# Turning queries and keys in 32x32 blocks on VectorE, with cluster masks placed by small transfers, in a routed-attention and feed-forward kernel

## The chip, the cores and the metric

The kernel runs on one core of a Trainium2 chip. The metric is device time in microseconds (us) of one execution. A profile of one execution shows five engines: PE (TensorE, matmuls; its weight loads are shown apart as PEld), DVE (VectorE), ACT (ScalarE), POOL (GpSimd) and SP (SyncE, which here only issues transfers). Each engine runs its own instructions strictly in the order in which the program lists them, and waits on semaphores for the others.

## The reference

Queries, keys and values have 4 batches, 8 heads, 768 tokens and 64 features. Each head has 16 cluster centroids; a query sees only keys of its own cluster. Behind the attention stands a feed-forward layer over 3072 tokens with a hard-swish gate.

```python
q_assign = np.argmax(np.einsum('bhsd,hcd->bhsc', q_n, c_n), axis=-1)
k_assign = np.argmax(np.einsum('bhsd,hcd->bhsc', k_n, c_n), axis=-1)
mask = q_assign[:, :, :, None] == k_assign[:, :, None, :]
scores = np.where(mask, scale * np.matmul(q, k.transpose(0, 1, 3, 2)), -1e9)
attn = softmax(scores);  x = np.matmul(attn, v)          # heads side by side: (3072, 512)
h = x @ w_in;  y = (h * np.clip(h + 3.0, 0.0, 6.0) / 6.0) @ w_out
```

## The kernel before

**Pairs of heads.** The 32 heads are worked on as 16 pairs `g` = 0 to 15 (two heads of one batch, 128 feature rows). Pairs 0 to 6 are computed as full attention (`FIRST` is 7, the eighth pair; `SECOND` is 8, the ninth). From pair 7 on, tokens are sorted by cluster and only a band of the scores is computed; those pairs are worked in between the feed-forward matmuls, from about 217 us on.

**The first stage** is a loop over `n`, in steps of two, of 12 key blocks for each of the seven pairs (`r = n % 12`). For each `n`, `scores` puts the masked scores of two heads into PSUM, by an f32 matmul on the turned data `xf` and a bf16 matmul on the mask `xm`; the first `n` of a pair starts with `xf`, all others with `xm`. `exponentials` (ACT) makes `ex`, `key_sums` adds these up in `acc` (POOL, in three places DVE), and `attn_v` multiplies with the values. `sum_up` (`pd`, at the third step of the next pair) sums `acc` over partitions.

**Preparing the next pair** is spread over the steps of the present one (`prep_items`). At `r` = 0 and 2, `turn` transposes queries and keys, loaded as tokens by features (`qk`), on PE: twelve 128x128 transposes into PSUM, copied to `xf` by ACT. At `r` = 4, `cluster_scores` (`pcs`) multiplies with the centroids, and ACT copies the result to `cs`. At `r` = 6, `route` turns `cs` on PE (`pr`, three transposes), and DVE takes the maximum (`mx`) and marks where it stands (`one_hot`). At `r` = 8 and 10, `route_turn` turns the marks back on PE (`po`, six bf16 transposes each) and ACT writes the mask `xm`. `count` (ACT) adds up the marks for a check of ties. The pairs 7 and 8 are turned in this stage too (`turn(FIRST, ...)` at `n` = 18 to 22; pair 8 at `n` = 72 and 74), with `own_clusters` and `order` in place of the masks.

**Weights.** The weights come as 64-bit floats, in 32 chunks of 512 KB (`raw`, three buffers). Each takes five DVE steps, one after another (L249, L255, L265, L271, L276), and two on ACT. They fill the rest of DVE: the list `decode` (160 such steps and four `weight_sums`) is worked off in portions that the function `share(n, r)` states for each step of the loop, after that step's preparation. A portion later in the list only starts when what stands ahead of it on DVE is done.

**The end of the stage.** From `n` = 64 on, the first feed-forward block runs too (`ph`, L660; ACT and DVE make the gate `g_sb` from it). At `n` = 84, `order(SECOND)` puts ranks into PSUM (`rk`), DVE multiplies them (L1142), and PE's next `pd` takes the same PSUM buffer.

**Queues.** The order on every engine is the order in which the program states it. SP issues the loads of `qk` (`load`, at `r` = 6), of values (`r` = 8), of weights, and the writes of the attention result (`xd<-num`). `qk` has one buffer. In the late stage, `load_natural` and `turn_blocks` already load and turn in blocks of 32x32: `rearrange` lets a transfer place 32x32 pieces such that DVE's transpose, which works on each block of 32x32 by itself, gives the whole turned matrix.

Of the kernel before, what the change touches and what calls it, by code (L numbers as in the profile page):

```python
# [8 lines left out]
F32 = mybir.dt.float32  # L9
# [8 lines left out]
C = 16  # L18
# [107 lines left out]
def fast_path(ctx, tc, ok, q, k, v, centroids, moe_w_in, moe_w_out, out):  # L126
# [44 lines left out]
    half_c = const.tile([P, 1], F32, name="half_c")  # L171
    cnT = const.tile([P, H * C], F32, name="cnT")
    one_hot = nump.tile([P, NC2, P], BF16, name="one_hot")


    plain = const.tile([P, FIRST * 2 * NCH], F32, name="plain")
# [20 lines left out]

    def load(g, *names):  # L200
        if g > FIRST or (g == FIRST and "v" in names):
            return
        if g == FIRST:
            g = SECOND
        b, h = divmod(2 * g, H)
        for name in names:
            if name == "v":
                dst = st["v", g] = vp.tile([P, 2, NCH, D], F32, name="vt")
            elif name == "q":
                if g == 1:  # L210
                    st["qk", g] = spare_rows(0)
                else:
                    st["qk", g] = qkp.tile([P, 2, NCH, 2, D], F32, name="qk")
            if name != "v":
                dst = st["qk", g][:, "qk".index(name)]
            src = {"q": q, "k": k, "v": v}[name]
            for t in range(2):
                queue = nc.scalar if (g, name, t) == (0, "q", 1) else nc.sync
                queue.dma_start((dst[:, t] if name == "v" else dst[:, :, t]), src[b, h + t].rearrange("(p j) d -> p j d", p=P))
# [103 lines left out]


    def turn(g, part, bank=None, held=None):
        if part == 0 and g == FIRST:
            st["xf", g] = spare[:, 2 * NC2 * P : 3 * NC2 * P].rearrange("p (n c) -> p n c", n=NC2)
        elif part == 0:
            st["xf", g] = xp.tile([P, NC2, P], F32, name="xf")
        qk, xf = st["qk", g], st["xf", g]  # L330
        pt = bank if bank is not None else scratch([P, 4, P], "pqk")
        for i in range(4):
            j = part * 4 + i
            if g == 0 and j == NCH:

                centroid_turn()
            nc.tensor.transpose(out=pt[:, i], in_=qk[:, j // NCH, j % NCH], identity=ident)
        dst = xf[:, part * 4 : part * 4 + 4]

        if g == 0 and part == 2:  # L340
            nc.vector.tensor_copy(out=dst, in_=pt)
        elif held is not None:
            held.append(lambda: nc.scalar.copy(out=dst, in_=pt))
        else:
            nc.scalar.copy(out=dst, in_=pt)
        if part == 2:
            st.pop(("qk", g))
# [4 lines left out]
    def cluster_scores(g):  # L352
        c0, xf = (2 * g) % H * C, st["xf", g]
        ps = scratch([P, 512], "pcs")[:, 0 : NC2 // 4 * P]
        for a in range(4):
            nc.tensor.matmul(  # L356
                ps[a * 2 * C : (a + 1) * 2 * C], lhsT=cnT[:, c0 : c0 + 2 * C], rhs=xf[:, a::4],
                start=True, stop=True,
            )
# [5 lines left out]
        nc.scalar.copy(out=cs, in_=ps)  # L365

    def route(g):
# [25 lines left out]

        later.append(count)

    def route_turn(g, part):
        if part == 0:
            st["xm", g] = xp.tile([P, NC2, P], BF16, name="xm")
        xm = st["xm", g]
        po = scratch([P, NCH, P], "po", BF16)  # L400
        for i in range(NCH):
            nc.tensor.transpose(out=po[:, i], in_=one_hot[:, part * NCH + i], identity=ident_q)
# [601 lines left out]
    Q = 32  # L1004

    def new_blocks(key):
        piece = st[key] = st["piecep"].tile([P, S], F32, name="piece")
        return piece

    def load_natural(g, a):  # L1010
        b, h = divmod(2 * g, H)
        blocks = new_blocks(("nat", g, a))
        for t in range(2):
            rows_ = (q, k)[a][b, h + t].rearrange("(r j c) (x i) -> x j c r i", j=Q, c=NCH, i=Q)
            for x in range(2):
                at = (2 * t + x) * Q
                nc.sync.dma_start(
                    blocks[at : at + Q].rearrange("p (c r i) -> p c r i", c=NCH, i=Q), rows_[x]
                )

    def load_sorted(g, a):
        blocks = new_blocks(("sorted", g, a))
# [414 lines left out]
    def prep_items(g, r):  # L1437

        if g > FIRST:
            return []  # L1440
        if g == FIRST:
            g = SECOND
        turns = [lambda part=part: turn(g, part) for part in range(3)]
        if g == SECOND:
            return {
                0: turns[:2], 2: turns[2:], 4: [lambda: cluster_scores(g)], 6: [lambda: own_clusters(g)],
            }.get(r, [])
        one_hots = [lambda: route_turn(g, 0), lambda: route_turn(g, 1)]
# [33 lines left out]
    def load_first():  # L1482
        b, h = divmod(2 * FIRST, H)
        st["qk", FIRST] = spare_rows(1)
        for a, x in enumerate((q, k)):
            for t in range(2):
                nc.sync.dma_start(st["qk", FIRST][:, a, :, t], x[b, h + t].rearrange("(p j) d -> p j d", p=P))
# [31 lines left out]
    with tc.manual_schedule():  # L1519
# [4 lines left out]
        load(0, "v")  # L1524
        load_weights(0)
        centroid_norm()
        for part in range(3):
            turn(0, part)
        idle(4)
# [14 lines left out]
        for n in range(0, total + lag_d + 2, 2):  # L1544
# [437 lines left out]
```

## Time and profile before

| what | value |
|---|---|
| median of 3 runs | 918.08 us (916.83 to 923.38) |
| the profiled execution | 917.25 us, of which the profile's span is 915.4 us |
| PE, PEld busy | 894.2 us (98%), 700.7 us (77%) |
| DVE, ACT, POOL busy | 581.9 us (64%), 304.2 us (33%), 602.9 us (66%) |
| seven pairs of the first stage | about 14 to 217 us |

A line of the windows view gives, for a stretch of the span, each engine's busy time with its count of instructions, then PE's granted clock (1.00 is full), the mean busy share of the DMA engines, and GB/s. A line of the timeline gives start, duration (of merged instructions, from the first to the last), engine, source line, operation and tiles. A line of the groups gives the busy time of a group, the mean duration of one instruction in ns, and the idle time just ahead of them with what ended it.

### The profile page before, as it was taken

How to read it: one execution, taken by the hardware profiler on the slowest of the kernel's cores; microseconds unless marked ns; L12 is line 12 of the kernel's file. 1: busy time of each engine (PE TensorE's matmuls, PEld its weight loads, DVE VectorE, ACT ScalarE, POOL GpSimd, SP SyncE). 2: the span in 40 equal slices, each digit the busy share in tenths (PEclk: the TensorE clock that was granted, in tenths of full speed). 3: DMA queues.
4: the chain of work that ended last, by engine and by line, in shares of the span. 5: the costliest groups of instructions: out<-in, count | busy, mean ns of one | idle time of the engine just before them, and what ended most of it. 6: DMA issues, size and time to landing. Idle time of an engine off the chain costs nothing.

```text
span 915.4 us, 17376 instructions
## 1 busy us (share of the span) xinstructions
PE 894.2 (98%) x6131; PEld 700.7 (77%) x6131; DVE 581.9 (64%) x1326; ACT 304.2 (33%) x627; POOL 602.9 (66%) x1438
## 2 busy tenths in 40 slices
PE   8999999997999999999999999999999999999997
PEld 5444445555788788797897887978978899999996
DVE  6775899777778378285594674765763645447461
ACT  6888786751221221322222131230321412112120
POOL 3877899995847848878878877788788461202030
PEclk9999999998999999999999999999999999999999
DMA  7756686526578467685785773965726344233210
GB/s 180 185 142 172 176 208 189 158 78 135 156 200 178 130 161 159 150 201 136 175 214 115 180 190 100 216 158 130 189 91 144 93 108 123 77 89 97 68 43 28
DMA packets 248249, 130.92 MB, mean 143 GB/s; under 512 B 206972, under 2 KB 225688, under 8 KB 248152
## 3 DMA queue, kind: packets, MB, share of 16 engines
q1 hardware_dynamic: 224184, 81.22, 37.0%
q10 hardware_dynamic: 13600, 34.31, 13.2%
q0 software_dynamic: 10368, 14.18, 5.0%
q8 instruction: 51, 0.84, 0.4%
q14 instruction: 46, 0.38, 0.1%
HBM read 99.69 MB, written 29.97 MB: 142 GB/s over the span
## 4 chain that ended last, share of the span: by engine, by line
PE 56%; DVE 4%; DMA 1%; issue 1%; another core or an unknown queue 0%; POOL 0%; ACT 0%; ACTq 0%
PE Y L758 15%; PE uY L719 13%; PE X L758 10%; PE uX L719 10%; PE pv L1300 2%; PE ps L1243 2%; PE pv L1243 1%; DVE g_sb L730 1%; DVE g_sb L541 1%; DVE sx L730 1%; PE pd L1324 1%; PE ps L1052 1%; PE pcs L356 1%; PE ps L1341 1%; DMA kvn<-in_k_dram 0%
## 5 line engine op out<-in xcount | busy, mean ns | idle before, releaser
L1213 POOL DMA_INDIRECT xn<-xsd,pos x108 | 109.5, 1014 | 59.1 <-PE uY L719 16.9
L538 ACT ACTIVATE sx<-g_sb,half_c 128x512 f32<-128x512 f32 x88 | 63.7, 724 | 199.6 <-DVE g_sb L730 160.7
L1162 POOL MEMSET unread<- 128x1 f32 x972 | 102.7, 106 | 37.6
L457 POOL TENSOR_TENSOR acc<-acc,ex 128x768 f32<-128x768 f32 x56 | 104.7, 1870 | 16.6 <-ACT ex L446 14.1
L1170 POOL DMA_INDIRECT qd<-qn,pos x96 | 99.2, 1034 | 19.9 <-issue 15.7
L703 POOL TENSOR_TENSOR g_sb<-g_sb 128x256 f32<-128x256 f32 x52 | 38.6, 764 | 111.0 <-DVE g_sb L541 110.0
L1170 POOL DMA_INDIRECT kvd<-kvn,pos x96 | 96.1, 1001 | 21.4 <-issue 21.4
L758 PE MATMUL X<-w_out_sb,g_sb 128*128 128x256 f32 x384 | 93.6, 388 | 1.5 <-issue 0.7
L719 PE MATMUL uX<-xb,w_in_sb 128*128 128x128 f32 x704 | 93.0, 275 | 0.0
L758 PE MATMUL Y<-T,g_sb 128*128 128x256 f32 x384 | 88.5, 381 | 0.0
L758 PE MATMUL Y<-w_out_sb,g_sb 128*128 128x256 f32 x384 | 88.4, 381 | 0.0
L719 PEld LDWEIGHTS uX<-xb,w_in_sb 128*128 128x128 f32 x704 | 85.7, 192 | 0.0
L758 PEld LDWEIGHTS X<-w_out_sb,g_sb 128*128 128x128 f32 x384 | 71.6, 193 | 17.2 <-issue 6.2
L758 PEld LDWEIGHTS Y<-w_out_sb,g_sb 128*128 128x128 f32 x384 | 72.1, 190 | 12.6 <-issue 2.7
L758 PEld LDWEIGHTS Y<-T,g_sb 128*128 128x128 f32 x384 | 71.9, 190 | 12.4 <-issue 2.7
L730 DVE TENSOR_TENSOR sx<-uX,sx 128x128 f32<-128x128 f32 x176 | 50.8, 288 | 42.5 <-ACT sx L737 30.4
L765 DVE TENSOR_TENSOR y<-y,Y 128x256 f32<-128x256 f32 x47 | 19.8, 421 | 86.1 <-PE Y L758 72.0
L423 PE MATMUL ps<-xf 64*128 64x384 f32 x336 | 68.8, 487 | 0.7 <-ACT ex L446 0.7
L730 DVE TENSOR_TENSOR g_sb<-uY,sx 128x128 f32<-128x128 f32 (+1 forms) x176 | 65.6, 414 | 0.0
L541 DVE SCALAR_TENSOR_TENSOR g_sb<-sx,g_sb 128x512 f32<-128x512 f32 x88 | 63.7, 726 | 2.0 <-ACT sx L538 1.0
L446 ACT ACTIVATE ex<-ps 128x768 f32<-128x768 f32 x84 | 63.7, 803 | 3.1 <-PE ps L423 2.6
L467 PE MATMUL pv<-ex,vt 128*64 128x384 f32 x336 | 63.5, 499 | 0.0
(230 smaller groups left out, 1717.8 us busy)
## 6 DMA issues: line engine op xcount, KB each, us to landing
tx<-td ACTq DMA_DIRECT2D x86, 384.0 KB
raw<-in_moe_w_in_dram SPq DMA_DIRECT2D x16, 512.0 KB
raw<-in_moe_w_out_dram SPq DMA_DIRECT2D x16, 512.0 KB
out_dram<-y SPq DMA_DIRECT2D x45, 128.0 KB
xb<-xd SPq DMA_DIRECT2D x11, 512.0 KB
piece<-qd SPq DMA_DIRECT2D x36, 96.0 KB
piece<-kvd SPq DMA_DIRECT2D x36, 96.0 KB
vs<-kvd SPq DMA_DIRECT2D x18, 192.0 KB
```

Source lines behind the costliest of these rows:

```text
L423: nc.tensor.matmul(st["ps", n][:, t, 0:HALF], lhsT=x[r, NCH + j], rhs=x[r, hf * NHC : (hf + 1) * NHC], start=first, stop=last, skip_group_ ...
L446: nc.scalar.activation(out=ex, in_=sc, func=ACT.Exp, scale=SM_SCALE)
L457: nc.gpsimd.tensor_tensor(out=acc, in0=acc, in1=ex, op=ALU.add)
L467: nc.tensor.matmul(pv[t * D : (t + 1) * D], lhsT=vt[:, t, j], rhs=ex[:, t], start=(j == 0), stop=(j == NCH - 1),)
L538: nc.scalar.activation(out=r, in_=h, func=ACT.Relu, bias=half_c, scale=1.0 / 6.0)
L541: nc.vector.scalar_tensor_tensor(out=g, in0=r, scalar=1.0, in1=h, op0=ALU.min, op1=ALU.mult)
L719: nc.tensor.matmul(dst, lhsT=w[:, kt], rhs=x(kt), start=(kt == 0), stop=(kt == HK - 1))
L730: nc.vector.tensor_tensor(out=out_, in0=in0, in1=in1, op=ALU.add)
L758: nc.tensor.matmul(bank[:, half * HC : (half + 1) * HC], lhsT=g_sb[:, kind, i], rhs=w[:, i], start=(first and i == 0), stop=(last and i == ...
L1162: nc.gpsimd.memset(unread, 0.0)
L1170: i = nc.gpsimd.indirect_dma_start(out=rows[name, g, t], in_=src[:, j, t].rearrange("p a d -> p (a d)") if a else src[:, j, t], in_offset= ...
L1213: nc.gpsimd.indirect_dma_start(out=xn[:, j, t], out_offset=None, in_=rows["xsd", g, t], in_offset=bass.IndirectOffsetOnAxis(ap=pos[:, 0, j ...
```

## The change

For pairs 2 to 8, queries and keys are loaded in 32x32 pieces (four transfers each for queries and for keys, of 768 pieces of 128 bytes, in place of two of 768 pieces of 256 bytes) and turned by one DVE instruction each, in place of twelve PE transposes and three ACT copies. For pairs 1 to 6, the cluster scores are turned by DVE (five instructions, with the maximum and the marks between them), and the mask goes from the work buffer `cs` into `xm` by eight small transfers on SP's queue, at `r` = 8. The mask buffers `xm` become two fixed ones, cleared once; queries load at `r` = 6 and keys at `r` = 8. The portions of weight decoding change: one step more in each of the pairs 0, 1 and 2 and two more in pair 3, five fewer in pair 6. Pair 0 is worked as before, and pair 1's queries and keys are still turned by PE.

```diff
+    def in_blocks(piece, g, a):
+        b, h = divmod(2 * g, H)
+        for t in range(2):
+            rows_ = (q, k)[a][b, h + t].rearrange("(r j c) (x i) -> x j c r i", j=Q, c=NCH, i=Q)
+            for x in range(2):
+                at = (2 * t + x) * Q
+                nc.sync.dma_start(
+                    piece[at : at + Q].rearrange("p (c r i) -> p c r i", c=NCH, i=Q), rows_[x]
+                )
+    def turn_early(g, a):
...
+        dst = st["xf", g][:, a * NCH : (a + 1) * NCH]
+        nc.vector.transpose(out=dst.rearrange("p j c -> p (j c)"), in_=st["qk", g][:, a])
...
     def cluster_scores(g):
...
-                ps[a * 2 * C : (a + 1) * 2 * C], lhsT=cnT[:, c0 : c0 + 2 * C], rhs=xf[:, a::4],
+                ps[a * 2 * C : (a + 1) * 2 * C], lhsT=cnT[:, c0 : c0 + 2 * C], rhs=part,
...
+    def mask_constants():
+        nc.gpsimd.memset(xms[1], 0.0)
+        nc.gpsimd.memset(counts[:, 1, 1:FIRST], -NC2 * (C - 1.0))
...
+    def block_route(g):
+        n = NC2 // 4 * P
+        cs = st.pop(("cs", g)).rearrange("p i c -> p (i c)")
+        by_token, oh = (
+            one_hot.rearrange("p j c -> p (j c)").bitcast(F32)[:, i * n : (i + 1) * n]
+            .rearrange("p (i c) -> p i c", c=C) for i in range(2)
+        )
+        nc.vector.transpose(out=by_token.rearrange("p i c -> p (i c)"), in_=cs)
+        mx = rtp.tile([P, n // C], F32, name="mx")
+        nc.vector.reduce_max(out=mx, in_=by_token, axis=AX.X)
+        nc.vector.tensor_tensor(
+            out=oh, in0=by_token, in1=mx.unsqueeze(2).to_broadcast([P, n // C, C]), op=ALU.is_ge
+        )
+        nc.vector.transpose(
+            out=by_token.rearrange("p i c -> p (i c)"), in_=oh.rearrange("p i c -> p (i c)")
+        )
+        ms, seen = (cs.bitcast(BF16)[:, i * n : (i + 1) * n] for i in range(2))
+        st["ms", g] = ms.rearrange("p (i c) -> p i c", c=P)
+        nc.vector.tensor_scalar(
+            out=ms, in0=by_token.rearrange("p i c -> p (i c)"),
+            scalar1=own[:, 0:1], scalar2=own[:, 1:2], op0=ALU.mult, op1=ALU.add,
+        )
...
+    def place_masks(g):
+        ms, xm = st.pop(("ms", g)), xms[g % 2]
+        st["xm", g] = xm
+        for a in range(4):
+            for t in range(2):
+                nc.sync.dma_start(
+                    xm[t * D : t * D + C, a // 2 * NCH : (a // 2 + 1) * NCH][:, a % 2 :: 2],
+                    ms[(2 * a + t) * C : (2 * a + t + 1) * C],
+                )
...
         return {
-            0: turns[:2], 2: turns[2:], 4: [lambda: cluster_scores(g)], 6: [lambda: route(g)],
-            8: one_hots[:1], 10: one_hots[1:],
+            0: turns[:1], 2: turns[1:], 4: [lambda: cluster_scores(g)], 6: [lambda: block_route(g)],
+            8: [lambda: place_masks(g)],
         }.get(r, [])
...
     def share(n, r):
         if n < 36:
-            return {0: 4, 2: 4, 4: 4, 6: 1, 8: 3, 10: 4}[r]
+            return {0: 4, 2: 4, 4: 4, 6: 1, 8: 4, 10: 4}[r]
         if n < 48:
-            return {0: 3, 2: 4, 4: 1, 6: 2, 8: 5, 10: 5}[r]
+            return {0: 4, 2: 4, 4: 2, 6: 2, 8: 5, 10: 5}[r]
...
-        return {0: 6, 2: 6, 4: 5, 6: 2, 8: 5, 10: 5}[r]
+        return {0: 6, 2: 6, 4: 4, 6: 2, 8: 4, 10: 2}[r]
...
     ranking = {
-        8: [load_first], 18: [lambda: turn(FIRST, 0)], 20: [lambda: turn(FIRST, 1)], 22: [lambda: turn(FIRST, 2)],
+        10: [lambda: load_first(0)], 14: [lambda: load_first(1)],
+        20: [lambda: turn_early(FIRST, 0)], 22: [lambda: turn_early(FIRST, 1)],
...
             if r == (4 if g == NKT else 6):
-                load(g + 2, "q", "k")
+                load(g + 2, "q")
             if r == 8:
                 load(g + 1, "v")
+                load(g + 2, "k")
```

More of the change, by code (lines that the diff above doesn't have):

```diff
@@ L173, in fast_path @@
     one_hot = nump.tile([P, NC2, P], BF16, name="one_hot")
+    xms = [nump.tile([P, NC2, P], BF16, name=f"xm{i}") for i in range(2)]
+    own = const.tile([P, 2], F32, name="own")
     plain = const.tile([P, FIRST * 2 * NCH], F32, name="plain")
@@ L325, in turn @@
     def turn(g, part, bank=None, held=None):
-        if part == 0 and g == FIRST:
-            st["xf", g] = spare[:, 2 * NC2 * P : 3 * NC2 * P].rearrange("p (n c) -> p n c", n=NC2)
-        elif part == 0:
+        if part == 0:
             st["xf", g] = xp.tile([P, NC2, P], F32, name="xf")
@@ L394, in route, with count @@
         later.append(count)
+    def mask_constants():
+        nc.gpsimd.memset(xms[1], 0.0)
+        nc.gpsimd.memset(counts[:, 1, 1:FIRST], -NC2 * (C - 1.0))
+        for a, (scale, bias) in enumerate(((1.0, 0.0), (FAR, -FAR))):
+            nc.gpsimd.memset(own[a * D : (a + 1) * D, 0:1], scale)
+            nc.gpsimd.memset(own[a * D : (a + 1) * D, 1:2], bias)
+    def block_route(g):
[20 more added lines that the diff above has]
+        )
+        def count():
+            nc.scalar.activation(
+                out=seen, in_=oh.rearrange("p i c -> p (i c)"), func=ACT.Copy, scale=0.5, accum_out=counts[:, 0, g : g + 1],
+            )
+        later.append(count)
+    def place_masks(g):
[6 more added lines that the diff above has]
+                    ms[(2 * a + t) * C : (2 * a + t + 1) * C],
+                )
     def route_turn(g, part):
         if part == 0:
-            st["xm", g] = xp.tile([P, NC2, P], BF16, name="xm")
+            st["xm", g] = xms[0]
         xm = st["xm", g]
@@ L1010, in load_natural @@
     def load_natural(g, a):
[L1011 to L1019, printed above, removed]
+        in_blocks(new_blocks(("nat", g, a)), g, a)
     def load_sorted(g, a):
@@ L1442, in prep_items @@
             g = SECOND
-        turns = [lambda part=part: turn(g, part) for part in range(3)]
+        turns = [lambda a=a: turn_early(g, a) for a in range(2)]
         if g == SECOND:
             return {
-                0: turns[:2], 2: turns[2:], 4: [lambda: cluster_scores(g)], 6: [lambda: own_clusters(g)],
+                0: turns[:1], 2: turns[1:], 4: [lambda: cluster_scores(g)], 6: [lambda: own_clusters(g)],
             }.get(r, [])
-        one_hots = [lambda: route_turn(g, 0), lambda: route_turn(g, 1)]
         if g == 1:
```

29 lines of the change are left out of this document (21 added, 8 removed).

## The prediction

> **What bounds the kernel now.** First the page's engine lines, then windows cut at the pairs' first masked scores, then who waited for whom.
>
> ```profile
> span 915.4 us, 17376 instructions
> PE 894.2 (98%) x6131; PEld 700.7 (77%) x6131; DVE 581.9 (64%) x1326; ACT 304.2 (33%) x627; POOL 602.9 (66%) x1438
> ...
> 34.10:58.60 24.50, 24.50 (x173) 11.54 (x175) 16.70 (x25) 20.79 (x43) 18.31 (x11) 1.00 0.66 185
> 58.60:83.80 25.20, 25.20 (x180) 11.00 (x178) 13.19 (x20) 21.69 (x45) 20.60 (x17) 1.00 0.51 147
> 83.80:109.10 25.30, 24.52 (x175) 10.86 (x171) 23.71 (x41) 19.55 (x40) 20.93 (x22) 1.00 0.57 158
> 109.10:133.80 24.70, 23.85 (x163) 10.35 (x163) 22.00 (x29) 21.67 (x46) 22.47 (x36) 1.00 0.66 182
> 133.80:169.40 35.60, 34.80 (x211) 19.71 (x211) 31.56 (x44) 24.35 (x53) 33.32 (x44) 1.00 0.71 199
> 211.60:216.20 4.60, 0.00 (x1) 0.03 (x1) 4.57 (x7) 0.11 (x1) 0.44 (x2) 0.94 0.84 210
> 216.20:222.50 6.30, 6.30 (x20) 4.08 (x21) 6.16 (x15) 0.48 (x1) 4.09 (x4) 0.50 0.43 106
> ```
>
> The five long rows are pairs 1 to 5. PE (first number behind the length) fills them to 97% and more, so PE bounds this stage and what it loses moves the end. But DVE (third) is at 22.0 of 24.7 us in pair 4 and 31.6 of 35.6 in pair 5: only pairs 1 and 2 have room. The last two rows are the stage's end: PE stands still for 4.6 us and then runs at half its clock for 6.3 us. DVE's own waits up to 182 us:
>
> ```profile
> DVE mx L374 <- PE pr L371: 15.3, 3, 7.2
> DVE g_sb L541 <- ACT g_sb L538: 5.5, 3, 2.5
> DVE mx L1074 <- PE pr L1072: 4.3, 1, 4.3
> DVE acc L454 <- ACT ex L446: 2.0, 2, 1.2
> DVE wtop L249 <- ACT xf L343: 0.4, 1, 0.4
> DVE acc L454 <- issue: 0.3, 1, 0.3
> ```
>
> Together 27.8 us (total, times, longest). More work than that cannot hide on DVE, as its order is fixed.
>
> **What PE loses.** From start to next start in the timeline of PE:
>
> ```profile
> 86.26 1.09 PE L337 MATMUL pqk<-ident,qk 128*128 128x128 f32 x8
> 87.29 0.34 PE L423 MATMUL ps<-xm 64*128 64x384 bf16 x2
> ...
> 91.23 0.66 PE L337 MATMUL pqk<-ident,qk 128*128 128x128 f32 x4
> 91.82 0.34 PE L423 MATMUL ps<-xm 64*128 64x384 bf16 x2
> ...
> 99.65 0.55 PE L371 MATMUL pr<-ident,cs 128*128 128x128 f32 x3
> 100.14 0.34 PE L423 MATMUL ps<-xm 64*128 64x384 bf16 x2
> ...
> 103.30 0.51 PE L402 MATMUL po<-ident_q,one_hot 128*128 128x128 bf16 x6
> 103.74 0.34 PE L423 MATMUL ps<-xm 64*128 64x384 bf16 x2
> ```
>
> Turning a pair takes 1.03 + 0.59 = 1.62 us, its clusters and masks 0.49 + 2 x 0.44 = 1.37 us. Seven turns and six masks: 11.3 + 8.2 = 19.5 us off PE. Nothing is added there: `cluster_scores` reads other columns, but as many.
>
> **What DVE gains.** Prices from the groups of DVE:
>
> ```profile
> L271 DVE SCALAR_TENSOR_TENSOR wunit<-raw,wunit 128x512 f32<-128x512 uint32 x32 | 35.7, 1117 | 1.0
> L265 DVE TENSOR_SCALAR wunit<-wtop 128x512 uint32<-128x512 uint32 x32 | 22.0, 689 | 0.8
> L380 DVE TENSOR_TENSOR one_hot<-pr,mx 128x192 bf16<-128x192 f32 x12 | 3.7, 353 | 0.4
> L374 DVE TENSOR_REDUCE mx<-pr 128x24 f32<-128x384 f32 x6 | 3.3, 554 | 15.4 <-PE pr L371 15.3
> L1080 DVE TENSOR_TENSOR oh<-pr,mx 128x384 bf16<-128x384 f32 x2 | 1.1, 558 | 0.1
> L1030 DVE STREAM_TRANSPOSE xsort<-piece 128x768 f32<-128x768 f32 x18 | 17.2, 965 | 9.8 <-DMA piece<-qd 5.6 <-DMA piece<-kvd 4.1
> ```
>
> - Turns: two transposes of 128x768 for each of seven pairs, the operation of L1030: 14 x (0.965 + 0.03 between instructions) = 13.9 us.
> - Masks: five instructions on 128x384, each near L1080's and L374's 0.56 us; the last, which the trace lacks, I take as 0.4. That makes 2.6 us, 2.7 with the gaps. L271, the decoding step that reads two SBUF tensors, averages 1.12 us where L265 takes 0.69; it stretches while POOL adds up `acc`. I take two such delays of 0.43 for each mask (the comparison reads two SBUF tensors; the scaling I count too): 3.6 us. Bounds: 2.7 without delay, 2.7 + 5 x 0.43 = 4.9 with one on each instruction. It replaces 0.55 + 2 x 0.35 = 1.3 us. Net 2.3 (1.4 to 3.6) each, six times 13.8 us (8.4 to 21.6).
> - Decoding steps brought ahead of pair 6: three in pairs 0 to 2, two in pair 3. A step averages (4 x 0.69 + 1.12)/5 + 0.03 = 0.81 us (the other three steps stand at 0.68 to 0.70 in the timeline lines below): 4.0 us.
>
> [...]
>
> **The sum.** PE meets DVE in each pair at two places: `pcs` needs the turned data, and the next pair's first scores need the masks. All of DVE's additions stand ahead of the turned keys of the ninth pair (`n` = 74), which PE needs for its last `pcs`:
>
> ```profile
> 181.07 0.69 DVE L249 TENSOR_SCALAR wtop<-raw 128x512 uint32<-128x512 uint32 x1
> ...
> 184.12 0.85 PE L356 MATMUL pcs<-xf,cnT 128*32 128x384 f32 x8
> ...
> 206.06 0.68 DVE L276 TENSOR_TENSOR w_out_sb<-wtop,wunit 128x512 f32<-128x512 f32 x1
> ...
> 207.51 0.70 DVE L255 SCALAR_TENSOR_TENSOR wtop<-raw,wtop 128x512 uint32<-128x512 uint32 x1
> ...
> 215.51 0.55 DVE L1142 TENSOR_TENSOR y<-rk,oh 128x384 f32<-128x384 f32 x1
> 216.20 1.51 PE L493 MATMUL pd<-acc,ones 128*32 128x384 f32 x8 [4.60 <-DVE y L1142]
> ```
>
> DVE ended the step that will stand just ahead of that transpose at 181.8 us. Without its waits that is 154.0; with 13.9 + 13.8 + 4.0 it is 185.7. PE alone would be there at 184.1 - 19.5 = 164.6. So DVE takes PE's place as the bound of the first 185 us, and the ninth pair's `pcs` comes at about 185.8: 1.7 us **later** than before. PE's 19.5 us go into waits at `pcs` and at the masks.
>
> Behind that, DVE has five decoding steps less and waits for PE again, so the last stretch stays with PE. Four of the five stood ahead of L1142, which kept PE waiting until 216.2: 4 x 0.7 = 2.8 us less, so the gap of 4.6 shrinks to about 1.8. The clock fell about 4.0 us after PE had stopped (in the 4.6 us row the mean is 0.94: half rate in its last 0.55 us). A gap of 1.8 ends before that, and the 6.3 us at 0.50 take 3.1 us less. [...]
>
> In all +1.7 - 2.8 - 3.1 = -4.2: 917.25 becomes 913.0 for this profiled execution; it lies 0.8 under the median of the runs, so I say **914 us**.
>
> **What lies beside.** ACT only loses copies, and has room in every row. POOL clears `xm` once at the start, before it has sums to add. The piece loads move the same 0.79 MB per pair in twice the pieces; rows of 147 to 199 GB/s are 3.7 to 7 MB per pair at shares of 0.51 to 0.71, so even double time for these bytes leaves the engines under full. The new wait is SP's, for DVE's last mask instruction; behind it on SP stand the write of `num` and the next weight chunk, which ACT and DVE read two chunks, some ten DVE steps or 8 us, later. The eight mask transfers cost little while SP issues freely:
>
> ```profile
> 45.70 3.40 SPq L219 DMA_DIRECT2D qk<-in_k_dram  x2
> ...
> 117.27 0.57 SPq L500 DMA_DIRECT2D sums<-dn  x1
> 118.97 0.32 SPq L510 DMA_DIRECT2D plain<-sums  x1
> ```
>
> A small transfer takes 0.57 us to issue and landed 1.1 us later (the next one waits for it): 8 x 0.57 + 1.1 = 5.7 us from mask to PE. [...]
>
> **Rivals.**
>
> *Masks free of POOL.* The two delays don't come, or POOL takes them: 6 x 0.9 = 5.4 us less, 908.4, and 907 if some L271 delays go too. For it: L265's unmoved 0.69. Against: L271's 1.12. Even with DVE idle the floor is PE's 917.25 - 19.5 - 5.9 = 892.
>
> *Slower: masks land late.* `pcs`, copy, DVE, eight transfers and the next pair's scores form a ring:
>
> ```profile
> 120.38 0.85 PE L356 MATMUL pcs<-xf,cnT 128*32 128x384 f32 x8
> ...
> 121.30 0.48 ACT L365 COPY cs<-pcs 128x384 f32<-128x384 f32 x1 [0.48 <-PE pcs L356]
> ```
>
> From pair 4's first mask (109.1) to its `pcs` PE takes 11.3 us, 9.7 without the turn; `pcs` and copy 1.4, DVE's portion ahead at most 4 x 0.8 = 3.2, the mask 3.6: 17.9 plus the transfers. DVE's own time for pair 4 is 27.0 us (24.7, less 2.0 of waits for `acc`, plus 2.0 and 2.3), so the ring decides once the transfers take over 9.1 us. At 14.7 it costs 5.6 us in each of three pairs, and PE, idle for over 4 us each time, drops to half clock: up to 3 us more for one of them. 17 to 20 us, with the rest of the sum unchanged about **932**. For it: the masks stand behind six larger loads on the same queue, and the row at 45.70. Against: the other issue times, and DVE being late leaves SP time to issue the loads before.
>
> *Slower by less: transposes wait for POOL as L271 does.* 14 + 12 transposes, of which the masks' 12 are half counted: about 20 x 0.43 = 8.6 us, 922.
>
> *The stage's end keeps its gap and clock* (DVE still late there): 919, inside my range.
>
> **How the numbers follow.** My own case 0.46, with 907 to 921 from the mask's bounds and the lost 5.9 at the end; masks free of POOL 0.22; masks late 0.22; transposes waiting 0.10. The range, 903 to 930, leaves out the full price of late masks and anything near PE alone. About 1% (9 us) is what a measurement of this kernel can tell from no change. Faster by more: most of the second case and the lower edge of mine, 0.23. Slower by more: most of the third and a little of the fourth, 0.21. The rest, 0.56, is the same.
>
> **What would show it.** Right: in pairs 1 to 5 DVE is busy for over 95%, its waits for PE nearly gone, while PE shows idle stretches of 2 to 6 us before `pcs` and before the first masked scores; the last `pcs` starts at 182 to 190 us; at the end the gap before `pd` is 1 to 3 us with the clock at 1.00. Wrong, if PE stays at 97% in pairs 3 and 4 (then the masks cost DVE less), if the mask instructions or transposes average far from 0.56 and 0.97 us, or if PE's waits end on transfers into `xm` while DVE idles (then the ring of the masks decides).

## The result: 3% slower, and the profile after

The changed kernel takes 943.7 us (median of 6 runs, 939.95 to 953.05) where the kernel before took 916.3 us beside it (911.9 to 923.4): a ratio of 1.0298, 95% interval 1.0254 to 1.0341. The prediction was 914 us, with a range up to 930. Medians below are over all runs; the ratios leave disturbed runs out, so kernels are compared by their ratios to the kernel before.

The engine lines of the page after; then the first stage in one window, after up to its last `pd` (240.9 us), and before up to its own (216.2 us).

```profile
span 939.1 us, 17142 instructions
PE 890.8 (95%) x5957; PEld 689.4 (73%) x5957; DVE 617.4 (66%) x1352; ACT 284.5 (30%) x582; POOL 605.2 (64%) x1444
```

```profile
14.00:240.90 226.90, 192.86 (x1105) 86.86 (x1103) 197.84 (x260) 129.82 (x266) 175.03 (x188) 0.92 0.54 142
```

```profile
14.00:216.20 202.20, 194.79 (x1276) 97.57 (x1273) 162.50 (x234) 150.46 (x311) 172.14 (x188) 1.00 0.56 157
```

The stage is 24.7 us longer, which is the whole loss (the span grew by 23.7). PE stands idle for 226.90 - 192.86 = 34.0 us instead of 7.4: 26.6 more. Its busy time fell by only 1.9 us although 19.5 us of work left it, because its mean clock is 0.92 instead of 1.00. What the busy time hides is 19.5 - 1.9 = 17.6 us of slow matmuls, and the clock row agrees: it is short of full by 0.08 x 226.9, some 18 us. 26.6 + 17.6 - 19.5 = 24.7. DVE is busy for 197.8 of 226.9 us (87%): not the bound that the prediction made of it. Whom PE waits for, after (us in total, times, longest):

```profile
PE ps L501 <- DMA xm<-cs: 21.1, 12, 5.9
PE ps L501 <- ACT ex L524: 4.7, 3, 3.9
PE pcs L387 <- DVE xf L223: 4.0, 2, 2.1
PE pd L571 <- DVE y L1210: 2.1, 1, 2.1
```

Most of the waiting, 21.1 us, is for the mask transfers. Windows cut at four of them and at the slow stretches behind them (PE busy is the first number behind the length, the clock the one behind the counts):

```profile
32.76:35.39 2.63, 0.00 (x1) 0.03 (x1) 2.53 (x4) 0.00 (x0) 2.55 (x2) 0.93 0.09 19
35.39:41.80 6.41, 6.00 (x18) 1.75 (x20) 6.24 (x10) 1.62 (x2) 3.10 (x2) 0.50 0.73 167
...
60.05:65.96 5.91, 0.01 (x1) 0.00 (x1) 5.77 (x8) 0.00 (x0) 2.84 (x2) 0.69 0.51 91
65.96:72.80 6.84, 5.95 (x18) 1.78 (x20) 3.46 (x6) 1.62 (x2) 1.75 (x1) 0.52 0.67 211
...
118.89:123.01 4.12, 0.01 (x2) 0.01 (x1) 3.92 (x7) 0.39 (x2) 3.93 (x6) 1.00 0.30 53
123.01:131.75 8.74, 8.11 (x30) 2.89 (x32) 7.82 (x12) 3.83 (x8) 6.06 (x13) 0.61 0.64 218
...
148.25:153.03 4.78, 0.01 (x2) 0.01 (x1) 4.58 (x7) 0.63 (x2) 4.43 (x7) 0.79 0.48 77
153.03:158.76 5.73, 5.31 (x16) 1.68 (x17) 1.65 (x4) 0.94 (x3) 4.87 (x6) 0.58 0.62 194
```

Each of these four waits is paid twice: 2.6 to 5.9 us of standing still, then 6 to 9 us at 0.50 to 0.61 of the clock, which costs 2.4 to 3.4 us more. Why the masks are late shows on the timelines of DVE and SP around the second of them:

```profile
53.45 1.83 DVE L452 TENSOR_SCALAR cs<-one_hot,own 128x384 bf16<-128x384 f32 x1
```

```profile
51.52 5.77 SPq L210 DMA_DIRECT2D blocks<-in_q_dram  x4
57.38 1.07 SPq L251 DMA_DIRECT2D vt<-in_v_dram  x2
58.50 2.94 SPq L210 DMA_DIRECT2D blocks<-in_k_dram  x4
61.55 5.55 SPq L469 DMA_DIRECT2D xm<-cs  x8
67.22 0.51 SPq L264 DMA_DIRECT2D raw<-in_moe_w_in_dram  x1
```

DVE has the mask at 55.28 us, and PE would take it at 60.05. SP is still issuing ten loads, starts with the first mask transfer at 61.55, takes 5.55 us for eight, and the last lands at 68.3: 13.0 us after DVE. In the other five pairs it was 8.2 to 9.7 us. And the next weight chunk (`raw`) stands behind all of that. What this does to the chunks shows where SP itself waits for VectorE to free a `raw` buffer, before and then after:

```profile
SPq L232 <- DVE wunit L271: 57.4, 18, 7.6
```

```profile
SPq L264 <- DVE wunit L303: 34.9, 9, 9.0
```

Before, SP often came to a load early and waited for its buffer; after, it does so half as often, since it comes late.

### The profile page after: what moved, and what is told of

It reads as the page before. It is cut to its first block, busy times and chain, and to the rows that moved or that the text cites. A ratio compares the mean times of both kernels' runs of the same rounds, so it can differ in the third digit from the quotient of the medians.

```text
span 939.1 us, 17142 instructions
## 1 busy us (share of the span) xinstructions
PE 890.8 (95%) x5957; PEld 689.4 (73%) x5957; DVE 617.4 (66%) x1352; ACT 284.5 (30%) x582; POOL 605.2 (64%) x1444
## 3 DMA queue, kind: packets, MB, share of 16 engines
q10 hardware_dynamic: 13600, 34.31, 12.9%
## 4 chain that ended last, share of the span: by engine, by line
PE 81%; DVE 8%; SPq 4%; DMA 3%; ACT 2%; issue 2%; another core or an unknown queue 0%; DVEq 0%; ACTq 0%
PE Y L836 18%; PE uY L797 16%; PE X L836 12%; PE uX L797 12%; PE ps L501 5%; PE pv L545 4%; PE pv L1368 3%; PE ps L1311 3%; SPq L469 2%; PE ph L738 2%; DMA raw<-in_moe_w_out_dram 1%; PE pcs L387 1%; PE pv L1311 1%; DVE y L1154 1%; PE pd L1392 1%
## 5 line engine op out<-in xcount | busy, mean ns | idle before, releaser
L535 POOL TENSOR_TENSOR acc<-acc,ex 128x768 f32<-128x768 f32 x56 | 106.8, 1907 | 17.1 <-ACT ex L524 14.3
L836 PEld LDWEIGHTS Y<-w_out_sb,g_sb 128*128 128x128 f32 x384 | 72.1, 190 | 12.6 <-issue 2.7
L501 PE MATMUL ps<-xf 64*128 64x384 f32 x336 | 74.2, 514 | 0.0
L545 PE MATMUL pv<-ex,vt 128*64 128x384 f32 x336 | 68.7, 533 | 0.0
```

Source lines behind the costliest of these rows:

```text
L501: nc.tensor.matmul(st["ps", n][:, t, 0:HALF], lhsT=x[r, NCH + j], rhs=x[r, hf * NHC : (hf + 1) * NHC], start=first, stop=last, skip_group_ ...
L535: nc.gpsimd.tensor_tensor(out=acc, in0=acc, in1=ex, op=ALU.add)
L545: nc.tensor.matmul(pv[t * D : (t + 1) * D], lhsT=vt[:, t, j], rhs=ex[:, t], start=(j == 0), stop=(j == NCH - 1),)
L836: nc.tensor.matmul(bank[:, half * HC : (half + 1) * HC], lhsT=g_sb[:, kind, i], rhs=w[:, i], start=(first and i == 0), stop=(last and i == ...
```

## The experiments

Three theories. A: the masks' own lateness is the price. B: VectorE's 28 us of added work are, and the waits for masks only stand where that shows. C, formed on the first four results: the issue time of SyncE (SP in the profile's lines) is what became scarce, and whatever stands behind its 18 transfers of a pair comes late, the weight chunks as well as the masks.

### 1. Taking the parts apart

`e1_no_transfers`:

```diff
-        for a in range(4):
+        for a in range(0):
             for t in range(2):
                 nc.sync.dma_start(xm[...], ms[...])
```

> The eight small mask transfers of each of six pairs are left out (the mask tiles keep what the first pair and a memset left in them, so the masks of pairs 1 to 6 are not those of the reference); VectorE's mask instructions, the turns in blocks and all else stay as in the changed kernel. Theory A (masks land late: in the changed kernel TensorE waits 21.1 us on the transfers into xm, and after five waits runs at 0.50 to 0.65 of its clock for 5 to 9 us each, together some 14 us): both go, the span falls from 939 to 903-916 us, TensorE's waits on xm are zero, and what is left of its idle time ends on VectorE's turns (pcs) or on raw loads. Theory B (VectorE's added 28 us are the bound, and the waits for masks only stand where VectorE's load shows): the time moves into waits for pcs and for exponentials, and the span stays above 928 us.

926.6 us, ratio 1.006 (1.003 to 1.009), span 925.3. By the ratios 2.4 of the 3.0% go, but the kernel is still no faster than before. PE's waits there:

```profile
PE pcs L387 <- DVE xf L223: 12.6, 3, 6.9
PE ps L501 <- ACT ex L524: 8.9, 7, 3.4
```

So the transfers are most of the price, and the span lies between the two forecasts. A second layer lies below: turns that are late on DVE.

`e2_turns_only` and `e3_masks_only`:

```diff
 e2:        -  6: [lambda: block_route(g)], 8: [lambda: place_masks(g)],
            +  6: [lambda: route(g)], 8: [lambda: route_turn(g, 0)], 10: [lambda: route_turn(g, 1)],
 e3:        -  turns = [lambda a=a: turn_early(g, a) for a in range(2)]
            +  turns = [lambda part=part: turn(g, part) for part in range(3)]   (and the loads in rows)
```

> Block loads and VectorE turns as in the changed kernel, with its shares of decode steps; cluster scores, masks and their turns by TensorE and ScalarE as in the kernel before. Theory A: TensorE keeps 11.3 us of the 19.5 us saved (seven turns at 1.62), no transfer stands between the masks and the scores, and the span is 904-917 us. Theory B: VectorE's 14 transposes of 0.97 us (13.6 us) already make it late, with waits before pcs in most pairs, and the span is over 922 us.

> Masks by VectorE and by eight transfers as in the changed kernel; queries and keys loaded in rows and turned by TensorE and ScalarE as in the kernel before; the changed kernel's shares. Theory A: the masks are late here too, a little less (four key and query issues on SyncE instead of eight, some 2.5 us less queue ahead of the masks), and TensorE is 11.3 us longer: 925-940 us. Theory B: VectorE carries only some 14 us more than before, and the span is 912-920 us.

Turns alone: 920.8 us, 1.0027 (0.9989 to 1.0065), not to be told from no change; the span, 922.4, is where B had it, but by one late turn, not by waits in most pairs. Masks alone: 930.3 us, 1.0078 (1.0025 to 1.0132), with a span of 920.8 between the forecasts. The two parts together should give 1.05%; the whole change costs 2.98%. The rest, some 18 us, needs both, which neither A nor B says: the two parts share something. The turns alone also show the second layer, a single wait in the timeline of PE, and then DVE's timeline ahead of it:

```profile
97.51 1.50 PE L387 MATMUL pcs<-xf,cnT 128*32 128x384 f32 x8 [7.10 <-DVE xf L223]
```

```profile
85.53 4.17 DVE L1154 TENSOR_TENSOR y<-y,oh 128x64 bf16<-128x64 bf16 x5
89.74 4.05 DVE L1154 TENSOR_TENSOR y<-y 128x64 bf16<-128x64 bf16 x4
...
96.48 0.97 DVE L223 STREAM_TRANSPOSE xf<-blocks 128x768 f32<-128x768 f32 x1
```

The keys' turn is stated at the pair's second step, behind the ordering of pair 7 (`run_up`, `step_up`; the forecasts below call it the seventh pair's) and four decoding steps, and DVE took them in that order: the turn began at 96.48 us, behind all of these.

### 2. Moving the order

`e4_masks_first`:

```diff
-            if r == 8: load(g + 1, "v"); load(g + 2, "k")      (ahead of the step's preparation)
+            if r == 8: load(g + 1, "v"); load(g + 2, "k")      (behind it)
```

> The changed kernel with one order turned round on SyncE: the mask transfers of a pair are issued ahead of the two value loads and the four key loads of the same step, not behind them. Theory A, queue part: the last mask then lands 8 x 0.64 + 1.8 = 6.9 us after VectorE's last mask instruction instead of 8 to 13 us; with the changed kernel's times of mask and need that leaves waits of 2.8, 2.1, 0.4, 4.8, 3.9 and 0 us, 14 us instead of 22, and two clock losses fewer: 924-932 us. If the small transfers themselves are the whole price (not the queue ahead of them), no change: 936-942 us. If SyncE, now held by VectorE, delays values and keys: over 942 us.

940.4 us, 1.022 (1.016 to 1.028), span 939.1, the forecast of "no change". But the waits on `xm` fell from 21.1 to 12.1 us, as the queue part said. The waits for exponentials rose from 4.7 to 13.0: SyncE stood waiting for VectorE's mask (13.9 us in all) with the weight chunks behind it, and ACT waited 27.1 us for chunks instead of 13.7. My third forecast had named values and keys as the victims; it was `raw`.

`e5_turns_at_once` (from the turns alone):

```diff
-            0: turns[:1], 2: turns[1:], 4: ...
+            0: turns, 4: ...
```

> The turns alone (masks by TensorE and ScalarE as in the kernel before), with one order changed: both turns of a pair stand at the pair's first step, so that the keys' turn is no longer queued on VectorE behind the seventh pair's ordering steps. Theory (a turn in VectorE's program order waits for whatever stands ahead of it): the 7.1 us wait before the cluster scores in the fourth pair of the turns-only kernel goes, and half of the 3.3 us of slow clock behind it: span 922.4 down to 911-916 us, 0.5 to 1% below the kernel before. Rival (VectorE is short of time there whatever the order): the wait moves to the next masks or scores of that pair, span 919-925 us.

913.7 us, span 911.3, ratio 1.0012 (0.9984 to 1.004). The 7.1 us wait is gone and no wait for `pcs` stands in its place; the span is what was forecast, but against the kernel before it is a draw, not the gain of 0.5 to 1%.

`e7_earlier` (from the changed kernel):

```diff
-            0: turns[:1], 2: turns[1:], 4: [cluster_scores], 6: [block_route], 8: [place_masks]
+            0: turns, 2: [cluster_scores], 4: [block_route], 6: [place_masks]     (ahead of load(g + 2, "q"))
```

> The changed kernel with the chain of a pair two steps (some 3 to 4 us) earlier: both turns at the first step, scores at the second, masks at the third, and the mask transfers ahead of the next queries' loads instead of behind values and keys; the decode shares of these steps exchanged. Theory A (the masks' chain is late by its place: 5.1 us of issue, 1.8 us of landing, and 2 to 6 us of queue ahead): the masks end 3 us earlier and land 6.9 us after that, so the waits on xm (21.1 us) fall under 5 us and the waits before pcs (4.0 us) go; span 912-924 us. Theory C (SyncE is short of time: 18 loads and transfers of 0.65 us a pair and the raw loads, each waiting in order): the waits move to raw loads and exponentials: 928-938 us.

934.8 us, 1.0225 (1.0168 to 1.0282), span 932.7, as theory C had it. The masks are now in time, and the waits are still there, under another name (waits of PE and of ACT, and ACT's timeline at the longest):

```profile
PE ps L501 <- ACT ex L524: 22.0, 8, 5.7
...
PE ps L501 <- DMA xm<-cs: 0.9, 3, 0.3
```

```profile
ACT wsize L277 <- DMA raw<-in_moe_w_in_dram: 23.8, 4, 7.4
ACT wsize L277 <- DMA raw<-in_moe_w_out_dram: 21.7, 5, 9.9
```

```profile
57.71 1.49 ACT L524 ACTIVATE ex<-ps 128x768 f32<-128x768 f32 x2
66.31 0.66 ACT L277 ACTIVATE wsize<-raw 128x512 bf16<-128x512 f32 x1 [7.11 <-DMA raw<-in_moe_w_in_dram]
66.97 1.49 ACT L524 ACTIVATE ex<-ps 128x768 f32<-128x768 f32 x2
```

ACT's step on a weight chunk stands ahead of the next exponentials. Its chunk is late, the exponentials behind it wait, and PE waits for those. In the kernel before, ACT waited 1.8 us for chunks in the whole stage.

### 3. Fewer issues, and another issuer

`e6_via_dram` and, with the earlier chain, `e10_earlier_dram` (the write at the fourth step, ahead of the queries, the reads behind them):

```diff
-        eight dma_start(xm[16 rows, 3 chunks], ms[16 rows])
+        nc.sync.dma_start(md, ms)
+        for t in range(2):
+            nc.sync.dma_start(wide[t * D : t * D + C], parts[t])     (md in DRAM)
```

> The changed kernel with the masks of a pair placed by three transfers instead of eight: one writes them to DRAM, two read them back into the mask tile (768 B runs; each fourth of the scores takes three adjacent columns of chunks). Same place on SyncE, behind values and keys. If the number of issues on SyncE (8 x 0.64 us a pair) is the price: 3.2 us less issue a pair, less one more landing of about 1.8 us on the way, so the masks land 1 to 2 us earlier, and the raw loads behind them 1 to 3 us earlier: 932-939 us of span. If only the place behind values and keys counts: 939 or more, since SyncE now waits for the first landing.

> The earlier chain of masks (turns at once, scores, masks and transfers each two steps earlier), with three transfers a pair by way of DRAM instead of eight: the write ahead of the queries' loads, the two reads behind them. SyncE issues 5 transfers fewer a pair, 3.2 us. Theory C: TensorE's 22.0 us of waits for exponentials (ScalarE held by raw loads) shrink by 8 to 16 us, the masks still in time: span 914-924 us against 932.7. Rival (raw loads are late because VectorE frees their buffers late, whatever SyncE does): 928-936 us.

By DRAM in the old place: 934.0 us, 1.0226 (1.0168 to 1.0285), span 931.3, just under the first forecast; waits on `xm` 14.9 instead of 21.1, but 9.4 instead of 4.0 for late turns. The gain on the changed kernel's 1.0298 is within the intervals. With the earlier chain: 914.5 us, **0.997** (0.9946 to 0.9994), span 913.3, as C had it, against 1.0225 for the earlier chain with eight transfers. There, five issues fewer in each of six pairs, with the reads behind the queries' loads, are worth 2.5%; the two were not taken apart. Its waits are 13.1 us for exponentials and 3.6 for masks, and ACT waits 29.2 us for chunks: what is left to win is mostly `raw`.

`e8_act_queue`: `nc.sync` becomes `nc.scalar` in `place_masks`.

> The changed kernel with the eight mask transfers issued by ScalarE's queue instead of SyncE's, at the same step. Theory C (SyncE's queue is what is short): raw loads, values and keys come 5.1 us a pair earlier and the masks no longer stand behind them: masks land 8 x 0.6 + 1.8 = 6.6 us after VectorE is done, waits on xm 21.1 -> 10 us, but ScalarE's issues (8 x 0.6 = 4.8 us a pair) hold the exponentials: 922-934 us. If ScalarE's exponentials are held by more than this (it waits in order for VectorE's mask), 935 us or more.

938.6 us, 1.0262 (1.0207 to 1.0317), as my last forecast had it. ACT needs 0.59 to 0.75 us for each issue and waits for VectorE first; PE waited 29.4 us for exponentials. The time of issuing did not vanish on another engine's queue.

`e11_earlier_none` (the earlier chain, `range(0)` in `place_masks`):

> The same earlier chain with no mask transfers at all (the mask tiles keep older contents, so the masks of pairs 1 to 6 are not those of the reference; VectorE's mask instructions stay). Theory C: no mask is waited for and SyncE has its 5.1 us a pair back, so the waits for exponentials fall from 22.0 us to under 8: span 906-916 us, which is what the change could bring if placing the masks cost nothing. Rival (VectorE's added load is the bound even so): 918-928 us.

916.4 us, 1.0002 (0.9971 to 1.0033), at the edge of what C forecast. It waits 8.5 us for exponentials, and 4.7 us before `pd`. So free placing alone would not have made the change a gain in this order: DVE is busy for 195.8 of the stage's 206.2 us (95%), and PE stands idle for 20.2. By way of DRAM, with the masks really placed, it was no slower (0.997): with three issues a pair, placing costs nothing that these runs can show.

### 4. SyncE's time by itself

`e9_idle_transfers` (in the turns at once, whose masks need no transfer) and `e13_before_idle` (in the kernel before):

```diff
+            8: [..., idle_transfers]
+    for each of eight blocks of 16 rows: nc.sync.dma_start(idle_to[rows, 3 x 40], ident_q[rows, 3 x 40])
```

> The kernel of the turns at once (masks by TensorE and ScalarE, 913.7 us), and beside its masks eight small transfers a pair on SyncE in the place where the changed kernel has its own, from a constant to a tile that nothing reads: 48 pieces each as there, but of 80 B. They wait for nothing and nobody waits for them; only SyncE's time is used. Theory C (SyncE's issue time is short; what it issues behind is late, raw loads first): TensorE's waits for exponentials grow by 5 to 15 us, with ScalarE waiting on raw loads: span 918-932 us against 911.3. Theory A alone (the masks' own lateness is the whole price, SyncE has time enough): 909-915 us.

> The kernel before with the same 48 idle transfers on SyncE, eight a pair, in the place of the changed kernel's masks (nothing waits for them). If SyncE is short of time only together with the block loads (eight issues of 0.65 us a pair instead of four): TensorE's waits for exponentials stay under 5 us and the time within 5 us of the kernel before. If eight small transfers hold up the raw loads in this kernel as much as in the turns at once: 12 to 17 us slower, with ScalarE waiting on raw loads as there (22 us).

In the turns at once: 928.3 us, 1.0123 (1.0082 to 1.0165), span 929.7, as C had it; it was 1.0012 without them. Nothing reads what they write. Timelines of SP, then of DVE, ACT and PE at the longest wait:

```profile
137.85 4.25 SPq L211 DMA_DIRECT2D blocks<-in_k_dram  x4
142.14 5.13 SPq L482 DMA_DIRECT2D idle_to<-ident_q  x8
147.38 0.52 SPq L265 DMA_DIRECT2D raw<-in_moe_w_out_dram  x1
```

```profile
151.39 0.69 DVE L282 TENSOR_SCALAR wtop<-raw 128x512 uint32<-128x512 uint32 x1 [4.87 <-DMA raw<-in_moe_w_out_dram]
...
151.31 0.67 ACT L278 ACTIVATE wsize<-raw 128x512 bf16<-128x512 f32 x1 [6.26 <-DMA raw<-in_moe_w_out_dram]
...
151.99 1.48 ACT L534 ACTIVATE ex<-ps 128x768 f32<-128x768 f32 x2
...
152.82 0.50 PE L511 MATMUL ps<-xm 64*128 64x384 bf16 x2 [6.63 <-ACT ex L534]
```

This is the suspected cost alone: 5.13 us of SP with a chunk behind it, DVE without work for 4.87 us, ACT for 6.26, and PE, which needs ACT's exponentials, for 6.63 and then at half clock (0.50 in the next 3 us; 0.50 us for two matmuls that took 0.33). In the kernel before, the same 48 transfers make it 921.0 us, 1.0075 (1.0035 to 1.0115): less, but not nothing. By the ratio, some 7 us, it lies between my two forecasts; by the medians (4.7 us) and PE's waits for exponentials (2.8 us) the first one holds. The masks alone cost as much (1.0078), but with 7.9 us of waits on masks in their profile, so that need not be the same cost.

### 5. What is left, and better versions

`e12_turns_best` (the turns at once; 22 and 26 decoding steps of two pairs shared out otherwise):

```diff
-        if n < 48: {0: 4, 2: 4, 4: 2, 6: 2, 8: 5, 10: 5}     if n < 60: {0: 5, 2: 4, 4: 4, 6: 2, 8: 5, 10: 6}
+        if n < 48: {0: 3, 2: 4, 4: 1, 6: 2, 8: 6, 10: 6}     if n < 60: {0: 5, 2: 4, 4: 3, 6: 2, 8: 6, 10: 6}
```

> The kernel of the turns at once with one decode step fewer at VectorE's queue ahead of the masks of the fifth pair, and one ahead of those of the sixth, given back later in the same pairs, and two fewer at the seventh pair's ordering. The waits of TensorE for VectorE's masks there (1.0 and 1.6 us) and for the ordering go in part: 1 to 3 us less than 911.3 us, 908-912. If VectorE simply has no time in these pairs the waits move on: 911-915 us.

912.0 us, **0.9961** (0.9934 to 0.9987), span 911.1, against 911.3 before the step: the best ratio here, though not by its stated step. The wait for the fifth pair's masks went, the sixth's grew from 1.6 to 3.2 us, the ordering's stayed at 2.8.

`e14_dram_late_k` and `e15_turns_late_k`: `load(g + 2, "k")` behind the decoding steps of the same step, in `e10` and in `e12`.

> The earlier chain with masks by way of DRAM, and the key loads of a step issued behind the raw loads of the same step's decode steps, not ahead of them. If the raw loads are late by their place behind four key issues (4 x 0.65 us and a wait of up to 3 us): TensorE's 13.1 us of waits for exponentials fall to 4-9 us, span 905-911 us against 913.3. If they are late since VectorE frees their buffers late, SyncE now waits for VectorE ahead of the keys, the keys' turn is late and the time is the same or longer: 912-922 us.

> The turns at once with the shares of the last kernel (912.0 us), key loads behind the raw loads of their step. TensorE waits only 2.6 us for exponentials there, so there is little to gain: 909-913 us; if the keys land late for their turn at the next pair's first step, 913-920 us.

922.7 us, 1.0081 (1.0047 to 1.0115), and 916.1 us, 1.000 (0.9974 to 1.0026), each as its second forecast had it. In `e14` the waits for exponentials fell from 13.1 to 7.6 us, so the place behind the keys was part of it; but SyncE then waits for VectorE ahead of the keys, masks and turns cost 2.8 us more of waits, and the slow clock takes 10.4 us of the stage instead of 5.1. Of the 8.2 us that the span grew, 4.4 lie behind the stage, where the edit changes nothing; those stay unexplained. No order that was tried is in time for all on one queue.

The issues of SP's queue between 14 us and the stage's end, counted in the traces, with their summed issue time. "Refills late" is the time from the last read of a `raw` buffer (by DVE or ACT) to the issue of the load that refills it, summed over the 29 refills:

| kernel | issues | us | refills late, us | PE idle, us | ratio |
|---|---|---|---|---|---|
| before | 109 | 64.6 | 25.6 | 7.4 | 1 |
| turns at once (e5) | 137 | 85.2 | 43.1 | 14.6 | 1.0012 |
| no transfers (e1) | 137 | 81.4 | 17.3 | 25.3 | 1.006 |
| by DRAM, earlier (e10) | 155 | 88.4 | 67.5 | 22.8 | 0.997 |
| by DRAM, old place (e6) | 155 | 90.3 | 63.8 | 32.5 | 1.0226 |
| before, idle transfers (e13) | 157 | 98.0 | 72.1 | 8.2 | 1.0075 |
| masks alone (e3) | 157 | 90.1 | 69.8 | 14.1 | 1.0078 |
| masks first (e4) | 185 | 118.2 | 120.2 | 29.5 | 1.022 |
| earlier, eight transfers (e7) | 185 | 114.2 | 132.4 | 30.3 | 1.0225 |
| turns, idle transfers (e9) | 185 | 114.9 | 117.5 | 26.4 | 1.0123 |
| changed kernel | 185 | 115.3 | 109.8 | 34.0 | 1.0298 |

The kernels with 185 issues, some 115 us in a stage of 217 to 227, are all slower by 1.2 to 3%, whether the transfers are needed or not, and their refills are the latest. The buffer is free by then, so it is the queue that is late, by issuing or by waiting for others, and not DVE that is late to free the buffer; between `e5` and `e9` only the 48 idle transfers differ. But the count is not all: `e6` is as slow as `e7` with 155 issues, since its masks and turns still come late in the old place (24.3 of its 32.5 us of idle time), and `e1` keeps 25.3 us of idle time with the refills in time, half of it before late turns. So the loss has two parts, late refills and a late chain of turn and mask, and these runs do not split it to the microsecond.

## Why the prediction was wrong, by its own steps

**What PE loses**: right as far as it can be seen. With the earlier chain by DRAM, PE is busy for 877.8 us over the span where it was 894.2 before; 16.4 of the 19.5 us are there even at a clock of 0.991.

**What DVE gains**: right in kind, and nearly in size for its own items. The groups of DVE in the stage, after:

```profile
L223 DVE STREAM_TRANSPOSE xf<-blocks 128x768 f32<-128x768 f32 x12 | 11.6, 969 | 0.0
L452 DVE TENSOR_SCALAR cs<-one_hot,own 128x384 bf16<-128x384 f32 x6 | 8.3, 1386 | 0.3
L444 DVE TENSOR_TENSOR one_hot<-one_hot,mx 128x384 f32<-128x384 f32 x6 | 5.0, 835 | 0.2
```

Transposes 0.969 us (0.965 taken). The five mask instructions sum to 3.9 us a mask (3.6 taken, 2.7 to 4.9 as bounds); the scaling is dearer than assumed, 1.39 us instead of 0.83, the comparison cheaper, 0.84 instead of 0.99. But DVE's busy time in the stage rose by 35.3 us, where turns and masks make 30: instructions that nobody changed became longer too, `y` (L1154) 11.6 us in all instead of 7.0 and `tx` (L677) 9.6 instead of 5.7. The sum had no term for that, and why they did was not tried.

**The sum**: its frame failed. It made DVE the bound, with PE meeting it at `pcs`; DVE now waits for others too, 12.9 us of it for weight chunks, for which it had never waited before, and is busy for 87%. With the transfers left out of the earlier chain (`e11`) the frame does hold: DVE is busy for 95%, PE's saving goes into waits, and the time is that of before.

**What lies beside** is the step that broke: "The eight mask transfers cost little while SP issues freely", with 5.7 us from mask to PE. Measured: 8.2 to 13.0 us, made of 0.5 to 6.3 us of queue ahead, 8 x 0.64 = 5.1 of issue (0.57 each was near) and, from the start of the last issue, 1.8 of landing (3.4 in one pair). The price of one issue was right: none of the 48 mask issues took over 0.74 us. The 10 issues of over 1 us in the stage before, one of the row at 45.70 among them, fell where the DMA engines were full (a mean share of 1.03). What was not done is the sum over the queue: 76 more issues in the stage, 51 us more of SP's time, on a queue on which each element waits for the one ahead (in `e4` the weight chunks stood behind 13.9 us of SyncE's waits for masks). "DVE being late leaves SP time" was the argument against it, and it did not come: in all six pairs SP reached the first mask transfer 0.5 to 6.3 us after DVE was done, and its waits for free `raw` buffers shrank from 57.4 to 34.9 us. The paragraph on block loads weighed bytes and the DMA engines, which indeed stay under full (0.54), and not the issuer.

**The rival of late masks** had the mechanism and the place, with a chance of 0.22. Its threshold of 9.1 us was too high: three of the five pairs that waited had transfers of 8.2 to 8.6 us. Its size was off too: it priced three pairs and "up to 3 us more for one of them" of clock, 17 to 20 us. The 14.7 us in it are eight issues at half of the 3.40 us that two took at 45.70 us, and 1.1 of landing; no run shows a mask issue at that price: the 48 took 0.59 to 0.74 us each. Waits came in five pairs, the four slow stretches shown above alone lose 12.3 us, and the late `raw` chunks were not in it: the stage lost 24.7 us.

**The end of the stage**: the gap before `pd` came as forecast, 2.1 us (1.8 taken), but the clock halved all the same:

```profile
238.00:240.90 2.90, 0.78 (x13) 0.57 (x14) 2.87 (x5) 0.00 (x0) 0.54 (x2) 0.81 0.86 237
240.90:242.40 1.50, 1.50 (x9) 0.27 (x9) 1.40 (x7) 0.00 (x0) 0.00 (x0) 0.50 0.99 214
242.40:246.00 3.60, 3.60 (x9) 2.88 (x10) 3.60 (x5) 0.48 (x1) 3.18 (x3) 0.50 0.23 77
```

PE had also stood for 1.16 us (236.82 to 237.98) ahead of the `rk` matmuls, 0.78 us of small work. The 3.1 us put down as saved were not: that a gap of 1.8 us keeps the clock was read from one row, in which the clock fell 4.0 us after PE had stopped. In the changed kernel's trace the clock fell 2.3 to 4.9 us after PE had stopped (the five waits of 2.6 us and more), so such a delay is not the same each time; the last section has where it fell.

## What to carry to other kernels

Before work is moved into transfers, add up the issuing engine's time as one does for a compute engine: number of issues times the issue time in the trace, and then ask what stands behind them in that queue. A load that was always early (here the weight chunks, for which ACT waited 1.8 us before and 13.7 us after) has hardly a row among the waits, and can be the first to be late. Where a transfer must be added, count the issues before the bytes: in the earlier chain three by way of DRAM beat eight direct ones by 2.5%. In the old place, where the masks still came late, they won 0.7%, which is within the intervals.

## What the runs showed of the hardware

- An issue of a small transfer held its queue for 0.59 to 0.61 us (median) whether it moved 48 pieces of 256 B (0.592 on SP in the changed kernel, 0.605 on ACT in `e8`) or of 80 B (0.593 on SP in `e9`). One issue is a third of the 1.8 us from its start to the landing, eight of them cost more in issue (5.1 us) than in landing, and 48 idle ones cost 1.1% of a kernel (`e9` against `e5`).
- The transposes of DVE took 0.965 to 0.972 us in all 14 places of the changed kernel's stage, though POOL's additions into `acc` ran beside ten of them in part or whole, and beside six for 87% or more of their time. The scaling, which reads one tensor in SBUF, took 0.48 us in the one place without such an addition and 1.18 to 1.95 beside one. Of the decoding step L271 before, which reads two, all 14 instances of over 1 us (1.18 to 2.31) had such an addition beside them for 53% or more of their time; the other 18 took 0.68 to 0.80, five of them beside additions for as long. No run shows what decides whether an instruction is held up.
- How short a wait costs the clock: of the isolated waits of PE in the first stage (no other of a microsecond within some 6 us), in all traces of this case, none of 6 between 1.0 and 1.4 us was followed by a lower clock (under 0.95 in the next 3 us), 18 of 36 between 1.4 and 2.7 us were, and all 40 of 2.75 us and more. The traces before and after show where the clock changes: in each, all changes (3 and 13) lie whole multiples of 3.41 us apart, as at 215.65 and 222.48 us before, and at 35.02, 41.84 and 62.32 us after. Cut on this grid, from 14 us to just behind the stage (225 us before, 250 after), the two have 115 stretches at full clock. Each of the 7 in which PE stood idle for 2.22 us or more was followed by half clock; none of the 5 with 1.19 to 1.69 us was, and none of the 103 under 1.0. So two short waits in one stretch added up (1.16 + 1.06 us from 236.40 to 239.82 us, at the end of the stage above), and a wait of 2.06 us that lay across a border (207.90 to 209.96 us after, 1.19 and 0.87 us on its two sides) was followed by full clock. A stretch need not be idle as a whole: 2.22 of its 3.41 us were enough. Between 1.69 and 2.22 us these two traces have no stretch.
